# Speech joint kernel on one core: engine programs in the plain streams, and the closing waits in order of issue

## Chip, cores and metric

The kernel runs on one core of one Trainium2 chip. The metric is the device time of one execution in microseconds, the median of several runs. Five engines take part, each with an instruction stream of its own: TensorE (PE), ScalarE (ACT), VectorE (DVE), GpSimd (POOL) and SyncE (SP). They know of one another through semaphores alone.

## The reference

Two convolutions over time, each of width 5 with a stride of 2 and a gelu, make `f` of 1000 steps out of 4000; it is projected, added to a projection of `g` for 8 labels, put through tanh and projected again. What is written is 2 x 1000 x 8 x 512 in bf16, 16.4 MB.

```python
def reference(x, w1, w2, g, w_f, w_g, w_o):   # x: 2 x 4000 x 512
    ...
    h = _gelu(h)[:, ::2, :]          # h: sum over 5 taps of x shifted @ w1[i]
    ...
    f = _gelu(f)[:, ::2, :]          # f: sum over 5 taps of h shifted @ w2[i]
    fe = jnp.einsum("btd,de->bte", f, w_f)
    ge = jnp.einsum("bud,de->bue", g, w_g)
    j = jnp.tanh(fe[:, :, None, :] + ge[:, None, :, :])
    return jnp.einsum("btud,dv->btuv", j, w_o)
```

## The kernel before

The work is a list of operations, each with what it reads and writes, and no engine program is written by hand. `Plan.op` and `Plan.dma` add to the list; `ORDER` at the top says, engine by engine, in which order the operations stand in that engine's stream, DMA issues among them; `Plan.edges` finds who must wait for whom, and `Plan.schedule` gives each operation a planned start time, kept in `self.start`. `Plan.emit` (line 236) then turns the list into instructions. Its inner function `run(name, e)` walks one engine's order, issues the waits that are not yet known to be met (`wait`, line 278 the instruction), then the operation, and lets it raise a semaphore.

The computation runs in stages: loads and transposes of `x`, the first convolution in row blocks of three outputs with fewer products than taps, the second likewise, the projection to `fe`, and from about half the span on the joint part: tanh on ACT into a ring of 256-column blocks, the last projection on PE in groups of four tiles of 128 rows with seven products in place of eight, evictions on ACT and DVE, sums for those products on POOL and DVE, and stores. A tile that belongs to no group of four is a plain one; its result lies in one of three tiles `ost` (written at lines 563, 568 and 453), a group's result in one of three tiles `og`.

Stores are issued at line 1030 (two tiles at once) and line 1040 (one tile or a part), nearly all from SP's queue. Two of the very last come from ACT's queue: the second half of the last group's two stores, and the last 128 columns of the last plain tile, behind the copy at line 453. Each place that stores come from has a semaphore of its own, eleven in all (`sems`, `s_o0` to `s_o10`, made as they are first used), raised by 16 for each store.

The engines' programs are put into a block: `nc.Block(no_gpsimd_drain=True)` is entered in the kernel function, and `emit` hands five functions to `@block.sync`, `@block.gpsimd` and so on (lines 296 to 312). Each engine gets a branch into its part at the start. When the block is left (the profile gives this line 360, that of the `with` statement), each engine goes to a common end, where PE, ACT, DVE and SP wait until they have drained, report to a semaphore, and wait for a release; POOL counts four reports and gives the release. A meeting of the same make stands at the very start of the program, before the block (the profile gives it line 1292, that of `_Bacc`); it belongs to the program's frame. Ahead of the closing meeting, SP waits until every one of the eleven store semaphores has its full count: the list `tail`, at the end of `run("sp", ...)`. The compiled program holds these as pairs on event semaphores, with the one left over on SP's branch to the common end, and turned round against the order of `sems`: 6 and 5, 7 and 4, 8 and 3, 9 and 2, 10 and 1, then 0.

Of the kernel before, what the change touches and what calls it, by code (L numbers as in the profile page):

```python
# [116 lines left out]
class Plan:  # L117
# [115 lines left out]
            assert len(done) > before  # L233
        return order

    def emit(self, block, tail):
        nc, ops = self.nc, self.ops
        pred = self.edges()
        order = self.schedule(pred)
        near = None  # L240
        for o in sorted((o for o in ops if o.port), key=lambda o: (self.start[o.idx], o.eng == "pool")):
            if o.eng == "dve":
                near = o.idx
            elif near is not None and self.start[near] > self.start[o.idx] - 1.5:
                o.after.append(near)
        pred = self.edges()
        pos = {i: p for e in order for p, i in enumerate(order[e])}
        deps = []
        for o in ops:
            need = {}  # L250
            for j, w in pred[o.idx].items():
                q = ops[j]
                if not w:
                    continue
                if q.dma:
                    need[("dma", j)] = j
                elif q.eng not in need or pos[need[q.eng]] < pos[j]:
                    need[q.eng] = j
            deps.append(need)
            for k, j in need.items():  # L260
                if not isinstance(k, tuple):
                    ops[j].signal = True
        cnt = {e: 0 for e in self.COMPUTE}
        sem = {e: nc.alloc_semaphore(f"s_{e}") for e in self.COMPUTE}
        for e in self.COMPUTE:
            for i in order[e]:
                if not ops[i].dma:
                    if ops[i].signal:
                        cnt[e] += 1
                    ops[i].count = cnt[e]  # L270

        def run(name, e):
            seen = {}

            def wait(s, v):
                if seen.get(id(s), 0) < v:
                    seen[id(s)] = v
                    e.wait_ge(s, v)

            for i in order[name]:  # L280
                o = ops[i]
                for k, j in sorted(deps[i].items(), key=lambda kj: -kj[1]):
                    if isinstance(k, tuple):
                        wait(ops[j].sem, ops[j].val)
                    else:
                        wait(sem[k], ops[j].count)
                ins = o.fn(e)
                if o.dma:
                    ins.then_inc(o.sem, 16)
                elif o.signal:  # L290
                    ins.then_inc(sem[name], 1)
            if name == "sp":
                for s, v in tail:
                    wait(s, v)

        @block.sync
        def _(e):
            run("sp", e)

        @block.gpsimd  # L300
        def _(e):
            run("pool", e)

        @block.tensor
        def _(e):
            run("pe", e)

        @block.scalar
        def _(e):
            run("act", e)  # L310

        @block.vector
        def _(e):
            run("dve", e)


def bass_standalone__seq2seq_rnn_t_joint__speech_kernel(
# [42 lines left out]
    with ExitStack() as es:  # L360
# [72 lines left out]
        kf = [at(f"kf{i}", [3, QH], FP32, v.end - v.bytes) for i, v in enumerate(ssum + ws[:2])]  # L433
        assert twf.end <= wv[3].end and sf.end <= xt[0].end and 3 * QH <= NT
        ps = Psum(es.enter_context(nc.psum_tensor("acc", [P, 8 * NT], FP32)))
        block = es.enter_context(nc.Block(no_gpsimd_drain=True))
        pl = Plan(nc)
        sub, add = ALU.subtract, ALU.add

# [351 lines left out]
        for m in range(NK):  # L791
            v = ps.cols(m * NT, ND).map(lambda a: a.rearrange("p (q r) -> p r q", r=6))
# [214 lines left out]
        sems = {}  # L1007
# [234 lines left out]
        for i, q in enumerate(seven):  # L1242
            p = seven[i - 1] if i else None
            base = min([(p or q).jt] + plains[:1]) * P
            last = i + 1 == len(seven)
# [29 lines left out]
        Plain(plains[1]).halves("dve", "sp")  # L1275
        end.part(slice(3 * P, NT), "act", "act")

        pl.emit(block, [(s[0], s[1]) for s in sems.values()])


# [26 lines left out]
```

## Time and profile before

| | |
|---|---|
| median of 3 runs | 250.69 us (250.52 to 250.94) |
| the profiled execution's own time | 250.55 us |
| its span, first to last instruction | 248.7 us |
| PE, DVE, ACT, POOL busy | 243.8, 208.0, 197.6, 100.7 us |
| granted TensorE clock | 1.00 |
| HBM read, written | 7.60 MB, 16.38 MB |
| last copy of a result starts (ACT, line 453) | 245.65 us |
| last store issued (ACT's queue, line 1040) | 245.96 us |

A row of the chain in order of time is start, duration and what ran. A row of a timeline is start, duration, engine, line, operation, output and input. A row of the view by line has engine and operation, the count behind an x, the shortest, median and longest duration in ns, and the start of the first and the last in us, rounded to a tenth. "SPq" is what SP's sequencer does itself: waits, drains, branches and DMA issues; "PEldq", "ACTq", "DVEq" and "POOLq" are the same of the other engines. A row of the waits is who waited at which line for whom: the sum in us, how often, the longest. The time of the profiled execution is longer than the span by what comes before the first instruction and after the last; the profile has no view of that.

### The profile page before, as it was taken

To read this page: it belongs to the slowest core of one execution; us is meant where nothing else is said; L and a number is where in the kernel's file an instruction comes from. 1 tells how busy PE (TensorE), PEld (TensorE's weight loads), DVE (VectorE), ACT (ScalarE), POOL (GpSimd) and SP (SyncE) were. 2 spreads that over 40 slices of the span, in tenths; PEclk is the share of its full clock that TensorE was granted. 3 is DMA by queue.
4 is the path that set the end of the run, shared out by engine and by line. 5 is a ranking of instruction groups with operands and counts; after the bars stand their busy time and mean duration, and the time that the engine had idled before them with its cause. 6 is when DMAs were issued, how large, how long until landed. Compare 5 with 4: busy or idle time off the path is not lost.

```text
span 248.7 us, 5271 instructions
## 1 busy us (share of the span) xinstructions
PE 243.8 (98%) x1938; PEld 182.6 (73%) x1944; DVE 208.0 (84%) x371; ACT 197.6 (79%) x349; POOL 100.7 (41%) x107
## 2 busy tenths in 40 slices
PE   7999999999999999999999999999999999999994
PEld 3879976666666666666566888777788878777883
DVE  1799996967999994796957889778999999996793
ACT  8787948458786475643699999999999999998672
POOL 1000000000000000000008988978799999999530
PEclk9999999999999999999999999999999999999999
DMA  6999999989000061000001043323345554454547
GB/s 212 319 224 179 126 209 173 193 169 355 31 3 0 0 209 48 0 4 0 0 3 42 31 147 106 100 87 127 109 156 161 172 188 162 160 182 137 192 153 249
DMA packets 54871, 31.83 MB, mean 128 GB/s; under 512 B 31902, under 2 KB 54590, under 8 KB 54846
## 3 DMA queue, kind: packets, MB, share of 16 engines
q1 hardware_dynamic: 54558, 31.34, 47.2%
q8 instruction: 15, 0.25, 0.5%
q10 hardware_dynamic: 288, 0.16, 0.2%
q14 instruction: 10, 0.08, 0.1%
HBM read 7.60 MB, written 16.38 MB: 96 GB/s over the span
## 4 chain that ended last, share of the span: by engine, by line
PE 86%; ACT 7%; DMA 2%; issue 1%; DVE 1%; SPq 0%; DVEq 0%; ACTq 0%
PE acc L461 86%; ACT jT L453 3%; DMA w_sb<-in_w_dram 2%; ACT sn L563 1%; ACT og L563 1%; ACT jX L453 1%; DVE og L448 1%; ACT sd L453 1%; DVE sn L564 0%; DVE og L564 0%; PE acc L599 0%; ACT fT L453 0%; SPq L479 0%; SPq L488 0%; ACT ost L453 0%
## 5 line engine op out<-in xcount | busy, mean ns | idle before, releaser
L448 DVE TENSOR_TENSOR og<-acc,sn 128x512 bf16<-128x512 f32 x84 | 54.7, 682 | 5.1 <-PE acc L461 5.1
L453 ACT ACTIVATE jT<-feT,geT 128x1000 bf16<-128x1000 f32 (+5 forms) x60 | 57.5, 1017 | 0.3 <-DVE feT L448 0.3
L1094 POOL TENSOR_TENSOR ss<-jT 128x512 f16<-128x512 bf16 x34 | 39.7, 1182 | 35.2 <-DVE ss L1094 33.3
L461 PE MATMUL acc<-tw,ss 128*128 128x256 f16 x336 | 46.0, 273 | 0.0
L461 PE MATMUL acc<-row,w_sb 128*128 128x334 bf16 (+2 forms) x224 | 39.2, 297 | 0.0
L461 PEld LDWEIGHTS acc<-tw,ss 128*128 128x128 f16 x336 | 32.3, 98 | 7.5 <-ACT sn L563 0.5
L461 PE MATMUL acc<-wo_sb,jT 128*128 128x256 bf16 (+1 forms) x205 | 33.1, 283 | 0.2
L563 ACT ACTIVATE sn<-acc 128x512 f32<-128x512 f32 x48 | 29.7, 628 | 3.4 <-PE acc L461 2.8
L564 DVE COPY sn<-acc 128x512 f32<-128x512 f32 x36 | 24.6, 685 | 6.3 <-PE acc L461 6.0
L453 ACT ACTIVATE hT<-acc 128x334 bf16<-128x334 f32 (+3 forms) x36 | 15.4, 430 | 17.4 <-PE acc L461 16.9
L461 PEld LDWEIGHTS acc<-row,w_sb 128*128 128x128 bf16 x224 | 21.2, 97 | 9.3 <-DVE acc L605 0.7
L453 ACT ACTIVATE sd<-acc 128x334 f32<-128x334 f32 (+2 forms) x48 | 20.5, 432 | 8.7 <-PE acc L461 7.4
L461 PEld LDWEIGHTS acc<-wo_sb,jT 128*128 128x128 bf16 x208 | 20.2, 98 | 5.1
L1094 POOL TENSOR_TENSOR ss<-ss,jT 128x512 f16<-128x512 f16 x19 | 22.3, 1179 | 2.4 <-DVE ss L1094 1.9
L445 POOL MEMSET hT<- 128x8 bf16 (+2 forms) x6 | 0.8, 148 | 55.5 <-ACT hT L453 43.0
L448 DVE TENSOR_TENSOR row<-row 128x1336 bf16<-128x1336 bf16 (+2 forms) x24 | 19.1, 806 | 0.0
L1094 POOL TENSOR_TENSOR ss<-jT,ss 128x512 f16<-128x512 bf16 x15 | 17.5, 1169 | 2.4 <-DVE ss L1094 2.4
L453 ACT ACTIVATE jX<-feT,geT 128x1000 bf16<-128x1000 f32 (+3 forms) x20 | 18.4, 965 | 0.0
L605 DVE SCALAR_TENSOR_TENSOR acc<-acc,sd 128x334 f32<-128x334 f32 (+2 forms) x24 | 11.7, 488 | 7.6 <-PE acc L461 7.5
L461 PE MATMUL acc<-xp,w_t 128*128 128x334 bf16 (+1 forms) x96 | 17.6, 305 | 0.0
L461 PE MATMUL acc<-hT,w_t 128*128 128x334 bf16 x96 | 17.6, 304 | 0.0
L461 PE MATMUL acc<-wo_sb,ss 128*128 128x256 bf16 x112 | 17.1, 273 | 0.0
(129 smaller groups left out, 473.4 us busy)
## 6 DMA issues: line engine op xcount, KB each, us to landing
out_dram<-og SPq DMA_DIRECT2D x42, 256.0 KB, 2.2
w_sb<-in_w_dram SPq DMA_DIRECT2D x10, 512.0 KB, 5.9
out_dram<-og SPq DMA_DIRECT2D x14, 128.0 KB, 2.3
out_dram<-ost SPq DMA_DIRECT2D x10, 128.0 KB, 1.9
xr<-in_x_dram SPq DMA_DIRECT2D x1, 512.0 KB, 3.2
wf_sb<-in_w_f_dram SPq DMA_DIRECT2D x1, 512.0 KB, 4.2
wg_sb<-in_w_g_dram SPq DMA_DIRECT2D x1, 512.0 KB, 5.2
wo_sb<-in_w_o_dram SPq DMA_DIRECT2D x1, 512.0 KB, 6.8
```

The source lines that it names most:

```text
L445: pl.op("pool", lambda e: e.memset(v.ap, 0.0), (), (v,))
L448: pl.op(eng, lambda e: e.tensor_tensor(out=o.ap, in0=a.ap, in1=b.ap, op=op), (a, b), (o,), 0.02 + 2.14e-3 * o.ap.free_size() if eng == "po ...
L453: pl.op("act", lambda e: e.activation(o.ap, i.ap, func, scale=scale, bias=0.0 if bias is None else bias.ap), rd, (o,), o.ap.free_size() * ...
L461: ins = e.matmul(o.ap, lhsT=l.ap, rhs=r.ap, start=start and n == 0, stop=stop and n == len(pairs) - 1, skip_group_check=not check)
L563: pl.flex({"act": (lambda e: e.activation(o.ap, v.ap, ACT.Copy), 0.05 + n * 0.833e-3), "dve": (lambda e: e.tensor_copy(out=o.ap, in_=v.ap) ...
L564: "dve": (lambda e: e.tensor_copy(out=o.ap, in_=v.ap), 0.065 + n * 1.04e-3)}, (v,), (o,))
L605: pl.op(eng, lambda e: e.scalar_tensor_tensor(out=o.ap, in0=a.ap, scalar=f, in1=b.ap, op0=ALU.mult, op1=add), (a, b), (o,), vec_cost(o, (a ...
L1094: fn = lambda e, o=S[i], x=x, y=y, op=op: e.tensor_tensor(out=o.ap, in0=x.ap, in1=y.ap, op=op)
```

## The change

The block is gone, with the branches at its start and the closing meeting. `emit` calls `run` for the five engines one after the other, on the engine objects themselves, so that every engine's instructions follow those that the frame has put into its stream. The list of closing waits, which SP still goes through, is sorted by the planned start of the last store that raises the semaphore; in the compiled stream there are then six event semaphores: 2; 1 and 7; 9 and 6; 10 and 5; 0 and 4; 8 and 3. The last store from ACT's queue raises number 8.

```diff
-    def emit(self, block, tail):
+    def emit(self, tail):
...
             if name == "sp":
-                for s, v in tail:
+                last = {id(o.sem): self.start[o.idx] for o in sorted((o for o in ops if o.dma), key=lambda o: self.start[o.idx])}
+                for s, v in sorted(tail, key=lambda sv: last[id(sv[0])]):
                     wait(s, v)
 
-        @block.sync
-        def _(e):
-            run("sp", e)
-
-        @block.gpsimd
-        def _(e):
-            run("pool", e)
...
+        for name, e in (("sp", nc.sync), ("pool", nc.gpsimd), ("pe", nc.tensor), ("act", nc.scalar), ("dve", nc.vector)):
+            run(name, e)
...
-        block = es.enter_context(nc.Block(no_gpsimd_drain=True))
...
-        pl.emit(block, [(s[0], s[1]) for s in sems.values()])
+        pl.emit([(s[0], s[1]) for s in sems.values()])
```

More of the change, by code (lines that the diff above doesn't have):

```diff
@@ L292, in run @@
             if name == "sp":
-                for s, v in tail:
+                last = {id(o.sem): self.start[o.idx] for o in sorted((o for o in ops if o.dma), key=lambda o: self.start[o.idx])}
+                for s, v in sorted(tail, key=lambda sv: last[id(sv[0])]):
                     wait(s, v)
-        @block.sync
-        def _(e):
-            run("sp", e)
-        @block.gpsimd
-        def _(e):
-            run("pool", e)
[L304 to L314, printed above, removed]
+        for name, e in (("sp", nc.sync), ("pool", nc.gpsimd), ("pe", nc.tensor), ("act", nc.scalar), ("dve", nc.vector)):
+            run(name, e)
 def bass_standalone__seq2seq_rnn_t_joint__speech_kernel(
```

## The prediction

> **What bounds the kernel now.** I read the page's busy rows and its chain first, then the chain in order of time at its end, then the instructions of the last 3 us by line, because everything that the change takes out stands in the first or the last microsecond.
>
> ```profile
> span 248.7 us, 5271 instructions
> PE 243.8 (98%) x1938; PEld 182.6 (73%) x1944; DVE 208.0 (84%) x371; ACT 197.6 (79%) x349; POOL 100.7 (41%) x107
> ...
> PE 86%; ACT 7%; DMA 2%; issue 1%; DVE 1%; SPq 0%; DVEq 0%; ACTq 0%
> ```
>
> TensorE is busy for 98% of the span and carries 86% of the chain. No edit touches an instruction that computes, or its place: put side by side, the two programs have the same matmuls, activations, vector operations and DMAs in the same order on every engine. They differ by the branches, and by what stands behind the last working instruction of each engine. So the middle of the span gives and takes nothing, and the sum is made at the two ends. The chain in order of time ends so:
>
> ```profile
> 242.61 3.01 PE acc L461 x23
> 245.62 0.03 issue
> 245.65 0.28 ACT ost L453
> ```
>
> and the timelines of ACT and SP, from 245.5 us on, and the out tensor's view, from 244 us on, have the last stores:
>
> ```profile
> 245.96 0.35 ACTq L1040 DMA_DIRECT2D out_dram<-ost  x1
> ```
>
> ```profile
> 245.87 0.33 SPq L1040 DMA_DIRECT2D out_dram<-ost  x1
> ```
>
> ```profile
> DMA to landing us min/median/max: 2.1/2.3/2.3
> ```
>
> Arithmetic ends at 245.93 us (245.65 + 0.28). ACT then issues the last store, 0.35 us long, at 245.96, and it lands 2.1 to 2.3 us after its issue began, between 248.06 and 248.26. The span goes on to 248.7. The waits of SP and its instructions at line 278 (the wait in emit) say which end of that it is; first SP's waits, then line 278 on SP from 244 us on, from 248 us on, and from 248.06 to 248.08 alone:
>
> ```profile
> SPq L278 <- DMA out_dram<-ost: 1.7, 1, 1.7
> ...
> SPq L360 <- PEq L360: 0.2, 1, 0.2
> ```
>
> ```profile
> L278 SPq EVENT_SEMAPHORE  x5: 28/28/28, 246.3 to 248.2; - x5
> ```
>
> ```profile
> L278 SPq EVENT_SEMAPHORE  x3: 28/28/28, 248.1 to 248.2; - x3
> ```
>
> ```profile
> L278 SPq EVENT_SEMAPHORE  x1: 28/28/28, 248.1 to 248.1; - x1
> ```
>
> SP waited 1.7 us for a store from ost. The wait that this store released runs at about 248.07 and takes 28 ns: 248.10 is the time at which SP knows that the output is out. What follows until 248.7 is bookkeeping, and line 360 (the end of the with statement, where the block closes) has it, engine by engine:
>
> ```profile
> L360 PEldq EVENT_SEMAPHORE  x2: 51/51/51, 245.7 to 248.7; - x2
> L360 DVEq EVENT_SEMAPHORE  x2: 21/21/21, 245.9 to 248.7; - x2
> L360 ACTq EVENT_SEMAPHORE  x2: 17/17/17, 246.5 to 248.7; - x2
> L360 SPq EVENT_SEMAPHORE  x2: 17/17/17, 248.5 to 248.7; - x2
> L360 POOLq EVENT_SEMAPHORE  x2: 17/17/17, 248.5 to 248.6; - x2
> L360 PEldq DRAIN  x1: 2048/2048/2048, 243.6 to 243.6; - x1
> L360 DVEq DRAIN  x1: 464/464/464, 245.4 to 245.4; - x1
> L360 ACTq DRAIN  x1: 167/167/167, 246.3 to 246.3; - x1
> L360 SPq COMPARE_BRANCH  x1: 41/41/41, 248.3 to 248.3; - x1
> L360 SPq DRAIN  x1: 7/7/7, 248.4 to 248.4; - x1
> ```
>
> and the same view of PE's queue from 248.67 to 248.69 alone:
>
> ```profile
> L360 PEldq EVENT_SEMAPHORE  x1: 51/51/51, 248.7 to 248.7; - x1
> ```
>
> PE, DVE and ACT reported to the meeting at 245.7, 245.9 and 246.5. They sat there until POOL, which counts the reports, had SP's (248.5) and released all of them (248.7). PE's release begins at about 248.68 and takes 51 ns, so the span ends at 248.73, which the page rounds.
>
> **The change, part by part.** The sum starts from the profiled execution: 250.55 us, of which 248.7 is span and 1.85 lies around it. The median of the runs is 250.69, 0.14 above; the same gain is taken off it.
>
> *Order of the closing waits.* Before, the compiled stream closes with five pairs of waits (the five rows of line 278) and has the eleventh wait on the branch of line 360. ACT's last store is waited for in the third pair: three of the five start from 248.07 on, so two pairs and the branch run behind it, at a step of (248.2 - 248.07) / 2 = 0.065 us. After, there are six event semaphores, and the last of them has that store. Gain: 2 x 0.065 = 0.13 us. If another store landed last, its wait would stand in front and one step would follow it: a loss of 0.065 at most.
>
> *The meeting.* Gone are the branch (a step after 248.2, at 248.26; the row says 248.3), SP's drain (248.4) and report (248.5), POOL's two semaphores (248.5 and 248.6) and the release (248.7). Order and meeting together reach from the end of the wait, 248.10, to the end of the span: 248.73 - 248.10 = 0.63 us, so the meeting's share is 0.50. Nothing hides this part: no engine computes after 245.93, and nobody waits for SP but the meeting. The drains of PE, DVE and ACT (2.0, 0.46 and 0.17 us) go as well, at no gain in the span: all end by 246.5, while SP is still waiting for the store.
>
> The cover is the transfer of the last stores, and it becomes the bound:
>
> ```profile
> 245.70:246.30 0.60, 0.00 (x0) 0.00 (x0) 0.14 (x1) 0.23 (x1) 0.00 (x0) 1.00 0.98 314
> 246.30:248.00 1.70, 0.00 (x0) 0.00 (x0) 0.00 (x0) 0.00 (x0) 0.00 (x0) 1.00 0.67 212
> ```
>
> These stretches (busy time of PE, PEld, DVE, ACT, POOL, then clock, DMA share and GB/s) are full of the stores of the last microseconds, and the change leaves their issue where it was.
>
> *The branches at the start.* Each engine loses a branch into its own block. The opening rows:
>
> ```profile
> L1292 SPq DRAIN  x1: 7/7/7, 0.0 to 0.0; - x1
> L1292 DVEq DRAIN  x1: 10/10/10, 0.1 to 0.1; - x1
> ...
> L1292 ACTq DRAIN  x1: 8/8/8, 0.1 to 0.1; - x1
> ...
> L1292 PEldq DRAIN  x1: 8/8/8, 0.3 to 0.3; - x1
> ...
> L1292 SPq EVENT_SEMAPHORE  x1: 17/17/17, 0.7 to 0.7; - x1
> ```
>
> ```profile
> 0.67 0.07 issue
> 0.73 0.39 SPq L488
> ```
>
> No record of a branch stands between the release (0.67, 17 ns) and the first load (0.73). What is left there is 0.07 - 0.017 = 0.05 us; the one branch that has a record takes 41 ns and the next instruction comes more than 0.1 later (248.3 to 248.4), which doesn't fit into 0.05. So the gain lies between 0 and 0.05, and I take 0. The Trainium skill, page "Advanced Engine Details and Errata", section "Control Flow Timing", puts a branch that is always taken at about 51 ns; by that the sum would be 0.05 larger, and no row here shows such a branch at the start.
>
> *Around the span.* 1.85 us lie outside, and no view shows them. Before, all five engines leave the program together at 248.6 to 248.7. After, PE leaves at 245.7, DVE at 245.9, ACT at 246.5 and POOL after 238.3 (its last operation):
>
> ```profile
> 237.18 1.16 POOL L1094 TENSOR_TENSOR ss<-jX,ss 128x512 f16<-128x512 bf16 x1
> ```
>
> Only SP comes at 248.1. Whatever the other four have to do on their way out is then done under SP's wait. The bounds: below, -0.63 (if leaving takes up again all that the meeting gave); above, +1.85 (nothing of the exit is SP's). The nearest row is the way in: SP reaches its first instruction at 0.0, DVE and ACT at 0.1, PE at 0.3. An exit that waits for SP alone, not for the slowest of five that start together, is shorter by about that spread. I take 0.3 us. It is the weakest term: an estimate by analogy from those drains.
>
> Sum: 0.13 + 0.50 + 0 + 0.3 = 0.93 us; 250.55 - 0.93 = 249.62 for the profiled execution, 250.69 - 0.93 = **249.76** for the median. Of it, 0.63 should be seen in the span: 248.1.
>
> **The rivals.**
>
> *The span's gain alone.* The exit takes 1.85 us from the moment that the last engine is through, whoever it is: 250.69 - 0.63 = 250.06. For it: a fixed piece around the span is the simplest reading of one execution. Against it: four of five engines have 1.6 us or more of lead (248.1 - 246.5), which they didn't have.
>
> *Taken up again.* Another meeting, outside the span, starts from something that SP's earlier end doesn't move, so the change doesn't do what it says: 250.69. For it: 1.85 us around the span is long, and something in it has to learn that five engines are through. Against it: that something can't be done before SP has ended, and SP ends 0.6 earlier. The Trainium skill, page "Runtime: NRT & Kernel Launch", section "The ~15µs preamble/postamble breakdown", has a sync barrier of about 1.5 us behind the kernel that waits for all engines; by this rule the engines meet a second time whatever the kernel does, and the sum would be 0.63 or more, since that barrier's wait ends with SP. No view here shows it.
>
> *Most of the exit hidden.* If about two thirds of the 1.85 are work of the four early engines, 1.2 goes in place of 0.3: 250.69 - 0.63 - 1.2 = 248.9. Against it: SP leaves by the same way, and needs some of it itself.
>
> *Slower: code loads against the last stores.* The queues that load instructions:
>
> ```profile
> q8 instruction: 15, 0.25, 0.5%
> ...
> q14 instruction: 10, 0.08, 0.1%
> ```
>
> A packet of q8 takes 0.005 x 16 x 248.7 / 15 = 1.3 us. Engines that no longer stop at the meeting run on into the code behind the program from 245.7 on, and load it while the DMA engines are 98% busy with the last stores. A store that finds two such packets ahead of one of its parts lands up to 2.7 us later: 250.69 + 2.7 - 0.93 = 252.4. It decides from a delay of 0.93 us, one such packet, on. Against it: PE's drain was taken up at 243.6, 2 us before its last matmul ended, so code is at hand well ahead of its use.
>
> **How the numbers follow.** Forecast (0.75 to 1.15 gained, 249.5 to 249.95) 0.50; span alone 0.25; taken up again 0.10; most hidden 0.09; slower 0.06. The likeliest case's time is 249.76. From 249.3 to 250.35 lie the forecast, the span alone with a spread of the runs of 0.2, half of the case between (a hidden part of 0.5 to 0.8) and little of "taken up again": 0.8. About 0.2%, 0.5 us, is what a measurement of this kernel can tell from no change. Faster by more: the forecast, the hidden exit and most of the span alone (0.63 stands only 0.13 beyond the bound), 0.50 + 0.09 + 0.21 = 0.80. Within 0.2%: 0.04 + 0.10 = 0.14. Slower: 0.06.
>
> **What would show each step.** In the changed profile the span should be 248.1, line 360's rows gone, and the last record an event semaphore of SP that starts about 248.1 behind a wait for ost's store. The first load should stay at 0.73; at 0.68 the branches had a price. PE's busy time should stay at 243.8 within 0.2, and the last store be issued at 245.96 within 0.2. The reported time less the span should fall from 1.85 to about 1.55; if it stays, the span alone was the whole gain, and if it rises to 2.5, the exit took it back. The prediction is wrong if the last store lands later than 248.3, or if an idle gap of PE over 0.3 us appears that before doesn't have.

## The result, and the profile after

The changed kernel takes 249.63 us (median of 6 runs, 249.20 to 249.75), against 250.57 us for the kernel before in the same series (6 runs, 250.28 to 250.94): 0.94 us between the medians. The ratio is 0.9955, 95% interval 0.9945 to 0.9966, so the changed kernel is faster, by a little under half a per cent. The interval stands for a gain of 0.85 to 1.38 us. The forecast was a gain of 0.93 us and a time of 249.76.

The profiled execution took 249.60 us. Its page, and SP's instructions at line 278 from 244 us on, from 248 us on and from 248.25 to 248.27 alone:

```profile
span 248.3 us, 5263 instructions
PE 245.0 (99%) x1944; PEld 183.4 (74%) x1944; DVE 206.5 (83%) x371; ACT 197.7 (80%) x349; POOL 101.4 (41%) x107
```

```profile
L278 SPq EVENT_SEMAPHORE  x6: 17/28/28, 246.4 to 248.3; - x6
```

```profile
L278 SPq EVENT_SEMAPHORE  x2: 28/28/28, 248.1 to 248.3; - x2
```

```profile
L278 SPq EVENT_SEMAPHORE  x1: 28/28/28, 248.3 to 248.3; - x1
```

There is no row left of the line where the block closed. The last record is the sixth wait of SP: it starts at 248.26 and with its 28 ns it ends the span, at 248.29. SP's waits at this line now are

```profile
SPq L278 <- DMA out_dram<-og: 0.9, 1, 0.9
SPq L278 <- DMA out_dram<-ost: 0.4, 1, 0.4
```

In place of one wait of 1.7 us for the last store and steps behind it, SP waits for one store after another as they land, and nothing follows the last. ACT's timeline has the last copy and the last store:

```profile
245.84 0.28 ACT L436 ACTIVATE ost<-acc 128x128 bf16<-128x128 f32 x1 [0.51 <-PE acc L444]
246.14 0.34 ACTq L1023 DMA_DIRECT2D out_dram<-ost  x1
```

From the issue of that store to the end of the span there were 248.73 - 245.96 = 2.77 us; now there are 248.29 - 246.14 = 2.15. That is the 0.63 of the prediction, to 0.01. But the span is only 0.4 shorter (248.7 to 248.3), because the last store was issued 0.18 later. The lateness is there after 29 us already (0.19), and the last copy is late by as much (245.84 against 245.65). The same four matmuls in the timelines of PE, before and after:

```profile
28.64 0.52 PE L461 MATMUL acc<-xa,w_x 128*128 128x206 bf16 x4
```

```profile
28.83 0.52 PE L444 MATMUL acc<-xa,w_x 128*128 128x206 bf16 x4
```

Outside the span lay 250.55 - 248.7 = 1.85 us; now it is 249.60 - 248.3 = 1.3. With the ends to a hundredth (248.73 and 248.29) it is 1.82 and 1.31. This part gave about 0.5, not 0.3.

### The profile page after: what moved, and what is told of

It is laid out like the page before. It is cut to its first block, busy times and chain, and to the rows that moved or that the text cites. A ratio compares the mean times of both kernels' runs of the same rounds, so it can differ in the third digit from the quotient of the medians.

```text
span 248.3 us, 5263 instructions
## 1 busy us (share of the span) xinstructions
PE 245.0 (99%) x1944; PEld 183.4 (74%) x1944; DVE 206.5 (83%) x371; ACT 197.7 (80%) x349; POOL 101.4 (41%) x107
## 4 chain that ended last, share of the span: by engine, by line
PE 99%; ACT 0%; issue 0%
PE acc L444 98%; PE acc L561 1%; PE acc L582 0%; ACT ost L436 0%
## 5 line engine op out<-in xcount | busy, mean ns | idle before, releaser
L1077 POOL TENSOR_TENSOR ss<-jT 128x512 f16<-128x512 bf16 x34 | 40.2, 1197 | 35.2 <-DVE ss L1077 33.3
```

Source lines behind the costliest of these rows:

```text
L1077: fn = lambda e, o=S[i], x=x, y=y, op=op: e.tensor_tensor(out=o.ap, in0=x.ap, in1=y.ap, op=op)
```

## The experiments

The reported time and the span are known for every run, so the time outside the span can be taken run by run, and its scatter is far smaller than that of the median. All runs, the span medians and the time outside as the median with its lowest and highest (the span is listed to a tenth):

| kernel | runs | median us | ratio to before, 95% | span us | outside us |
|---|---|---|---|---|---|
| before, second series | 26 | 250.69 | | 248.9 | 1.78 (1.74 to 1.84) |
| changed | 6 | 249.63 | 0.9955 (0.9945 to 0.9966) | 248.3 | 1.32 (1.30 to 1.35) |
| changed, again | 6 | 249.63 | 0.9962 (0.9948 to 0.9977) | 248.3 | 1.33 (1.28 to 1.36) |
| all four held | 12 | 250.18 | 0.9984 (0.9973 to 0.9995) | 248.35 | 1.83 (1.79 to 1.87) |
| block, new order | 10 | 250.67 | 1.0000 (0.9989 to 1.0011) | 248.9 | 1.80 (1.74 to 1.83) |
| no block, old order | 7 | 249.75 | 0.9962 (0.9949 to 0.9976) | 248.4 | 1.30 (1.26 to 1.35) |
| DVE held | 4 | 249.62 | 0.9937 (0.9915 to 0.9959) | 248.2 | 1.43 (1.37 to 1.47) |
| ACT held | 10 | 249.93 | 0.9962 (0.9945 to 0.9979) | 248.45 | 1.47 (1.43 to 1.54) |
| PE held | 6 | 250.10 | 0.9964 (0.9946 to 0.9982) | 248.5 | 1.58 (1.54 to 1.62) |
| POOL held | 10 | 250.14 | 0.9970 (0.9953 to 0.9986) | 248.3 | 1.86 (1.80 to 1.89) |
| SP later | 10 | 250.53 | 0.9986 (0.9972 to 1.0001) | 249.2 | 1.33 (1.27 to 1.35) |

The runs come from four series, each with runs of the kernel before beside it, the last three on a chip each of their own: "changed" is that of the result (before: 250.57); "changed, again", "all held" and the two kernels on the order are the second; the rows of DVE, PE and POOL held and of SP later are the third (before: 21 runs, 250.76 us, 1.78 outside); ACT held is the fourth (before: 13 runs, 250.98 us, 1.79 outside). A ratio is to the kernel before of the same series and is not the quotient of the two medians. The time outside of the kernel before is the same in all three series that list it, so it can be compared between series; the medians differ by some tenths for the kernel before alone.

**The changed kernel again**, no edit.

> The changed kernel once more, unaltered, for its spread. Theory A (early leaving): PE, ACT, DVE and POOL leave the program 1.6 us or more ahead of SP and do their part of the exit under SP's last wait. It expects the time outside the span again near 1.3 us (first run 249.60 - 248.3) and the median at 249.6 +- 0.2. The 0.18 us by which ACT's last store was issued later (246.14 against 245.96) is jitter of the opening loads by both theories: it should be another number here, between -0.3 and +0.3 against 245.96. If it is 246.14 again within 0.05, the change itself has moved the middle.

The last row of ACT's timeline:

```profile
246.33 0.35 ACTq L1023 DMA_DIRECT2D out_dram<-ost  x1
```

The time outside is the same, 1.33. The last store was issued at 246.33 this time, neither 246.14 nor 245.96, so the change hasn't moved the middle to a fixed new place; but it is 0.37 after 245.96, outside the 0.3 that was expected. Over all profiles of this study that issue lies between 245.96 and 246.43; with the block it was 245.96 and 246.26, without it 246.03 to 246.43. So 0.18 in one pair of profiles is within the jitter between executions, though only two of these profiles have the block. The medians of the spans, 248.9 in 26 runs and 248.3 in 6 and 6, give the 0.6 that the two profiles hide. Less what passes from the last store's issue to the end (2.77 and 2.15), they put that issue at about 246.1 (an estimate) with the block and without.

**All four held.** No block, but the engines that have nothing left to do wait for the last stores as SP does:

```diff
+            if name in ('pe', 'act', 'dve', 'pool'):
+                last = {id(o.sem): self.start[o.idx] for o in sorted((o for o in ops if o.dma), key=lambda o: self.start[o.idx])}
+                for s, v in sorted(tail, key=lambda sv: last[id(sv[0])])[-3:]:
+                    e.wait_ge(s, v)
```

> No block and no meeting, but PE, ACT, DVE and POOL each end on waits for the last stores (three of the semaphores that SP waits for last), so that all five engines leave together, when the last store has landed. Theory A: the span stays about 248.3, and the time outside it rises from 1.3 back to 1.7 to 1.9; median about 250.1 to 250.2. Rival B (the meeting's own leavings): the 0.5 us outside the span that the change saved belonged to the closing meeting's drains, branch and semaphores; those are still gone, so the time outside stays 1.3 and the median 249.6.

The added waits, by line, and the page's span:

```profile
L299 ACTq EVENT_SEMAPHORE  x2: 17/28/38, 248.0 to 248.2; - x2
L299 POOLq EVENT_SEMAPHORE  x2: 17/30/43, 248.0 to 248.2; - x2
L299 DVEq EVENT_SEMAPHORE  x2: 21/36/50, 248.0 to 248.2; - x2
L299 PEldq EVENT_SEMAPHORE  x2: 51/51/51, 248.0 to 248.2; - x2
```

```profile
span 248.2 us, 5271 instructions
```

All five engines end at 248.2, and the reported time is 250.04: 1.8 outside, over 12 runs 1.83. There is no drain, branch or report in this kernel, so rival B falls: what the change saves outside the span is not a leaving of the meeting, it is the head start of the four engines. It doesn't lie ahead of the first instruction either, since this kernel has no block at its start. Theory A's numbers (1.7 to 1.9; 250.1 to 250.2) hold.

**The order alone**, in the kernel before, and **the old order**, in the changed one:

```diff
-                for s, v in tail:
+                last = {id(o.sem): self.start[o.idx] for o in sorted((o for o in ops if o.dma), key=lambda o: self.start[o.idx])}
+                for s, v in sorted(tail, key=lambda sv: last[id(sv[0])]):
```

> The block with its closing meeting as before, only the closing waits sorted by the planned start of the last store. By the prediction's step: the last store's wait stands one step ahead of the branch in place of three, so two steps of 0.065 us are gained: from the issue of ACT's last store (start of its row) to the end of the span 2.64 us in place of 2.77, the time outside the span unchanged at 1.85; median about 250.45. Rival B expects the same here. If the order were the larger part of the gain, the median would come below 250.0.

With the block and the new order, the last store's row, then lines 278 and 362 (the block's close) on SP, the release of PE alone (from 248.85 to 248.86), then the span:

```profile
246.26 0.35 ACTq L1042 DMA_DIRECT2D out_dram<-ost  x1
```

```profile
L278 SPq EVENT_SEMAPHORE  x2: 28/28/28, 248.2 to 248.4; - x2
```

```profile
L362 SPq EVENT_SEMAPHORE  x2: 17/17/17, 248.7 to 248.8; - x2
L362 SPq COMPARE_BRANCH  x1: 41/41/41, 248.4 to 248.4; - x1
L362 SPq DRAIN  x1: 7/7/7, 248.6 to 248.6; - x1
```

```profile
L362 PEldq EVENT_SEMAPHORE  x1: 51/51/51, 248.9 to 248.9; - x1
```

```profile
span 248.9 us, 5277 instructions
```

The branch follows the last wait at once. PE's release starts between 248.85 and 248.86 and takes 51 ns, so the span ends at about 248.91. From the store's issue that is 2.65 us, where 2.64 was expected, and the time outside stays at 1.80. The median missed the expected 250.45: it is 250.67 beside 250.69 for the kernel before. It can't tell the two apart, since 0.13 us is less than the interval (0.9989 to 1.0011).

> No block, no meeting, but the closing waits in their old order. The last store's wait is then the fourth of six event semaphores and two steps follow: from the issue of ACT's last store to the end of the span 2.27 us in place of 2.14, the time outside as in the changed kernel, 1.3; median about 249.75. If the order had carried the gain, it would be near 250.4.

The same rows of the changed kernel with the old order; here the diff above is taken back:

```profile
246.38 0.35 ACTq L1022 DMA_DIRECT2D out_dram<-ost  x1
```

```profile
L278 SPq EVENT_SEMAPHORE  x3: 28/28/28, 248.5 to 248.6; - x3
```

```profile
span 248.7 us, 5263 instructions
```

The wait that the last store releases is at 248.5, two more follow. The last of them starts at 248.62 and ends the span at 248.65, which is 2.27 after the issue. So the two steps cost 0.12 to 0.13 in either surrounding, and the order's share is as the prediction had it: small, and lost in the scatter of the runs' times.

**One engine held at a time**: the edit of "all four held" with one name in the tuple.

> Of the four engines that leave early only PE is held until the last stores have landed; POOL, ACT and DVE leave early as in the changed kernel. With all four held the time outside the span rose from 1.3 to 1.83 us. Theory A1 (the prediction's analogy with the way in, where PE comes last): PE carries it, time outside 1.7 to 1.85, median 250.1. Theory A2 (POOL is the slow one on the way out): PE costs less than half, time outside 1.4 to 1.6, median about 249.85.

> Only POOL is held until the last stores have landed. Theory A1: time outside stays at 1.3 to 1.4, median 249.65. Theory A2: POOL carries nearly all of it, time outside 1.7 to 1.85, median 250.1.

> Only DVE is held until the last stores have landed. Theories A1 and A2: it is no slow one on the way in (0.1 us), so it costs little: time outside 1.3 to 1.45, median 249.65 to 249.75. If each engine costs the same, whichever it is (theory A3: the exit starts anew whenever one more engine is late), it costs 0.5 as well.

> Only ACT is held until the last stores have landed, to complete the row: time outside the span was 1.33 us with none held, 1.43 with DVE, 1.58 with PE, 1.86 with POOL. If each engine has a way out of its own and the slowest held one sets the time, ACT's cost lies between DVE's 0.1 and POOL's 0.53, and as it comes on the way in with DVE (0.1), I expect 1.45 to 1.6, median about 249.8.

The held engine's rows, PE, POOL, DVE and ACT in this order, each from its own kernel:

```profile
L299 PEldq EVENT_SEMAPHORE  x2: 51/51/51, 248.0 to 248.2; - x2
```

```profile
L299 POOLq EVENT_SEMAPHORE  x2: 17/30/43, 248.3 to 248.4; - x2
```

```profile
L299 DVEq EVENT_SEMAPHORE  x2: 21/36/50, 248.3 to 248.4; - x2
```

```profile
L299 ACTq EVENT_SEMAPHORE  x2: 17/28/38, 248.2 to 248.4; - x2
```

The spans of these profiles are 248.2, 248.5, 248.5 and 248.4, so each engine was held to the end of the span. Against 1.33 with none held, the time outside grows by 0.10 for DVE, 0.14 for ACT, 0.25 for PE and 0.53 for POOL. POOL alone costs what all four cost (1.86 and 1.83): the costs don't add, and the runs read as if the slowest way out decided. Theory A2 holds; A1, the prediction's reason, falls, though its size for PE (0.3) is near to what PE costs. ACT at 1.47 is inside what was expected, and A3 is out. These theories are judged by the time outside alone. The median of PE held, 250.10, is the one that A1 expected (A2: 249.85), because the spans of these six runs are long (248.5); ACT held missed as well (249.93 for 249.8).

One reading is left untested: that an engine's cost comes from the two instructions added at its end and not from its lateness. No run adds them to POOL without holding it. Against it stands the kernel before, where POOL ends late on other instructions and the time outside is 1.78.

**SP later.**

```diff
                 for s, v in sorted(tail, key=lambda sv: last[id(sv[0])]):
                     wait(s, v)
+                for _ in range(16):
+                    e.wait_ge(s, v)
```

> SP goes through eight more event semaphores on counts that are met already, so that thirteen steps of 0.065 us follow the last store's wait (some waits of the old list are paired with the added ones): SP ends 0.85 us later. Theory A: the exit hangs on SP alone, so span and time both rise by 0.85: median 250.45, time outside 1.3. Rival C (the exit has a part that runs from the other engines' end and is not over when SP ends): the time rises by less than the span, and the time outside falls below 1.2.

```profile
L297 SPq EVENT_SEMAPHORE  x14: 17/28/28, 248.5 to 249.3; - x14
```

The row has fourteen event semaphores on the last store's count, thirteen steps from 248.5 to 249.3: 0.8 us, or about 0.06 each. The span's median rises by 0.9 (249.2 against 248.3), the time by 0.90 (250.53 against 249.63), the time outside not at all (1.33). What the medians have beyond 0.8 is within the scatter between series (250.76 against 250.69 for the kernel before). Rival C falls: with the other four out, what SP's end is late the kernel's time is late.

## Why the prediction was right, and where it was not

*What bounds the kernel.* Right: nothing in the middle moved by the change. Two of the marks that the prediction set, PE's busy time within 0.2 of 243.8 and the last store at 245.96 within 0.2, were set from one execution and are narrower than the scatter of executions. The second is met in the first profile (246.14) and missed in the repeat (246.33). The changed kernel's profile misses the first (245.0), with all of its 1944 matmuls recorded where before had 1938; the kernel with its block and the new order has as much:

```profile
PE 244.9 (98%) x1944; PEld 183.0 (74%) x1944; DVE 208.1 (84%) x371; ACT 197.8 (79%) x349; POOL 101.1 (41%) x107
```

The sign of being wrong, a last store that lands later than 248.3, has the same weakness. In the changed kernel's profile SP's wait ends just inside it, at 248.29, but with the block and the new order it starts at 248.4 and with the old order at 248.5, each time because the store was issued later (246.26 and 246.38). No idle gap of PE over 0.3 us came up: the longest piece of "issue" in the changed kernel's chain is 0.05 us.

*Order of the waits*, 0.13: right, shown from both sides (2.77 to 2.65, and 2.27 to 2.15).

*The meeting*, 0.50: right. With the order it makes 0.63 from the last store's issue to the span's end (2.77 to 2.15), and 0.6 in the medians of the spans. The predicted span of 248.1 was not seen, 248.3 was, because it was reckoned from an execution that reached its last store early.

*The branches at the start*, 0: right. The first load starts where it did, in SP's timeline:

```profile
0.74 0.39 SPq L471 DMA_DIRECT2D xr<-in_x_dram  x1
```

No gain of 0.05 is seen there. That is the figure that the Trainium skill, page "Advanced Engine Details and Errata", section "Control Flow Timing", would have given for a branch that is always taken.

*Around the span*, 0.3: the sign and the mechanism (the four engines do their part of the exit under SP's wait) are right, and shown (all four held: back to 1.83), but the term was too small. It is 0.45 to 0.5: 1.78 to 1.33 in the medians, 1.82 to 1.31 in the two profiles. The step that failed is the analogy with the way in: "An exit that waits for SP alone, not for the slowest of five that start together, is shorter by about that spread." It took PE, at 0.3, for the slowest and left POOL out. In size the spread is near for PE (0.3 in, 0.25 out), DVE (0.1 and 0.10) and ACT (0.1 and 0.14); that the two have one cause isn't shown. It fails for POOL, which costs 0.53 on the way out. Its opening rows before are

```profile
L1292 POOLq INC_SWDGE_SEM  x1: 27/27/27, 0.1 to 0.1; - x1
L1292 POOLq DRAIN  x1: 186/186/186, 0.3 to 0.3; - x1
```

Its first record is at 0.1, as early as DVE's and ACT's. Its drain, the kind of row that the prediction took for the other engines, starts at 0.3 like PE's and lasts to about 0.5. That end is near 0.53, but four memsets stand beside the drain, which no view has at the way out, and nothing here ties the two together.

That the sum came out at 0.93 against 0.94 in the first series is luck. The term outside was too small by about 0.15, and the six runs of the kernel before in that series have a median 0.12 below that of the 26 in the second (250.57 and 250.69). In the second series the medians are 1.06 apart (250.69 and 249.63), which is 0.6 in the span and 0.45 outside.

*The rivals.* The span's gain alone is out: 250.06 was its time, and the time outside fell. Taken up again is out, and SP later shows why: with the other four out, the rest follows SP's end one to one. Holding any one of the four raises the time outside (1.43 to 1.86 against 1.33), so something outside the span depends on every engine. The Trainium skill, page "Runtime: NRT & Kernel Launch", section "The ~15µs preamble/postamble breakdown", has a sync barrier behind the kernel that waits for all engines; the runs agree with that, and no view shows the barrier itself. Most of the exit hidden is out: 1.3 us are left. The slower rival, code loads against the last stores, left no mark: the last store's issue to the end of its wait took 248.10 - 245.96 = 2.14 before and 248.29 - 246.14 = 2.15 after.

## What to carry to other kernels

A closing meeting of all engines costs twice: its own steps behind the last store (0.5 us here), and the head start on the way out that it takes from the engines which are done (0.45 us here), most of all POOL's. Let each engine end as soon as its own work has ended, let SP alone wait for the stores, and let the wait for the one that lands last be the last. To judge tenths of a microsecond, measure from a fixed event (here the last store's issue) and split the time into span and rest; the span scatters from run to run by more than the effect (248.3 to 249.6 in the 26 runs of the kernel before).

## What was not expected of the hardware

POOL's way out is the longest of the four that can leave early: with POOL ending together with SP, the time outside is 1.86 us, with POOL some 10 us ahead and one other engine late beside SP 1.43 to 1.58, and with SP alone late 1.33. POOL's last computing instruction started at 237.18 us before, so its way out costs nothing if nothing holds it (with all four let go the time outside is 1.33). Why POOL's lateness costs 0.53 us, no view here shows. After the last store's issue 2.1 us pass until SP knows that it has landed, with the block and without (248.10 - 245.96 and 248.29 - 246.14); the change leaves this, and it is now the whole of the span's end.
